# Part 1 of a gated linear attention and FFN kernel in units of two chunks and four heads, with the decays summed on TensorE

## The chip, the cores and the metric

The kernel runs on one core of one Trainium2 chip. The metric is the device time of one execution in microseconds (us). The kernel before takes 508.98 us, median of four runs (507.14 to 509.68). The profiled execution is one of these runs; its span, 506.9 us from the first to the last instruction, is about 2 us shorter than its time.

Runs more than 1.5% above the fastest of their kernel are called slow, and ratios leave them out.

## The reference

```python
# q, k, v, alpha: (B, H, S, D) = (4, 8, 768, 48) float32; alpha in 0.8 .. 1.0
for t in range(S):
    state = alpha[:, :, t, :, None] * state + einsum('bhd,bhe->bhde', k[:, :, t], v[:, :, t])
    y[:, :, t] = einsum('bhd,bhde->bhe', q[:, :, t], state)
x = y.transpose(0, 2, 1, 3).reshape(B * S, H * D)        # 3072 x 384
a, b = x @ w1, x @ w2                                    # w1, w2: 384 x 1024, float64
out = ((a * b) @ w3) @ w_out                             # w3: 1024 x 1024, w_out: 1024 x 384, float64
```

The recurrence is computed in chunks. Within a chunk, `k` is divided by the product of the `alpha`s so far and `q` is multiplied by it; the outputs are then masked scores times `v` (called attend below) plus `q` times the state that enters the chunk. The products of `alpha` are sums of logarithms: a matmul with a triangular matrix of ones, then `exp`. The FFN's matmuls are done with operands split in three parts, and the float64 weights are converted to float32 on the core, on VectorE and ScalarE ("conversions").

## The kernel before

Part 1 is the attention. It goes through 24 units of one chunk (128 positions, one on each partition) with all 8 heads. Between the units it converts the FFN's gate weights (12 blocks) and, from round 5 on, computes gates of token groups that are already finished. Part 2 computes the rest of the gates, folds `w3 @ w_out` and projects.

The loads fetch, for each head and position, the 48 floats of one row, which is 192 bytes:

```python
def rows(src, n):
    b, c = divmod(n, NCH)
    return src[b, :, ds(c * C, C), :].rearrange("h p d -> p h d")     # 192 B runs
```

The sums are one matmul of all 384 features, in two parts (one part, in fp32, in the first ten units), and the decay of the state from chunk to chunk makes a trip by way of DRAM, because it is needed with the features on the partitions and `e` has the positions there:

```python
for i in range(2):
    nc.tensor.matmul(lc, sums[:, n % 2], la[:, i], start=(i == 0), stop=(i == 1))
nc.scalar.activation(e[:, 0], lc, AF.Exp, scale=-1.0)
nc.scalar.activation(e[:, 1], lc, AF.Exp)
if n in ends:                                            # every second chunk
    nc.scalar.dma_start(out=ends[n][0:1], in_=e[0:1, 0])
...                                                      # load_ends: ends -> decs, 4 B runs
```

All psum tiles come from one pool of eight banks. The order of a round is this:

```python
for n in range(N + 1):
    load_v(n + AHEAD - 1); load_a(n + 5); load_kq(n + AHEAD)
    attend_state(n - 1)          # q times the state, into y
    scores(n)
    transposed(n + 1)            # q, k with features on partitions
    ...                          # split_x of a finished group, conversions
    advance(n)                   # decay times state, on GpSimd
    attend(n - 1)                # adds into y; ScalarE copies y out; DMA to DRAM (xd)
    outer(n)                     # k times v, the state's increment
    run(...)                     # a piece of a gate
    decayed(n + 2); logs(n + 4)
    if n in begin: load_x(...)   # a finished group comes back from DRAM
    decays(n + 3); load_ends(n + 2)
```

In these listings calls are put on one line and guards are left out.

## Time and profile before

| | before |
|---|---|
| time, median | 508.98 us |
| TensorE busy | 466.6 of 506.9 us |
| VectorE / ScalarE busy | 371.3 / 248.1 us |
| gaps with no matmul (work is what is left) | 40.2 us |
| TensorE work done at half clock | 18.8 us |
| scores of round 10 / 23 begin at | 106.3 / 205.8 us |

Work and gaps are counted here from the matmul records in the trace: from each matmul's start to the next one's start is work, apart from the time in which no matmul runs, which is a gap. The page's summary lines for the kernel before, and its line for packets and for the queue that carries the loads:

```profile
PE 466.6 (92%) x3760; PEld 424.8 (84%) x3760; DVE 371.3 (73%) x620; ACT 248.1 (49%) x479; POOL 13.8 (3%) x43
...
DMA packets 168735, 79.10 MB, mean 156 GB/s; under 512 B 112856, under 2 KB 162544, under 8 KB 168688
...
q1 hardware_dynamic: 147184, 70.73, 54.9%
```

Two thirds of the packets are under 512 bytes.

### The profile page before, as it was taken

The numbers are of one execution on the slowest core, as the hardware profiler recorded it, in microseconds if no ns is written. First come the engines' busy times: TensorE is split into PE (matmuls) and PEld (weight loads), VectorE is DVE, ScalarE is ACT, GpSimd is POOL, SyncE is SP. The second block draws the span as 40 slices with busy tenths as digits, with TensorE's granted clock in tenths as the row PEclk, the third lists the DMA queues.
The fourth block names the chain that finished last, engine by engine and source line by source line (L and its number), as shares of the span: only waits on it lengthen the run. The fifth ranks groups of instructions, "written<-read, shape, count | busy, mean of one in ns | idle before, by whom it ended". The sixth has DMA issues, their size and how long they took to land.

```text
span 506.9 us, 9883 instructions
## 1 busy us (share of the span) xinstructions
PE 466.6 (92%) x3760; PEld 424.8 (84%) x3760; DVE 371.3 (73%) x620; ACT 248.1 (49%) x479; POOL 13.8 (3%) x43
## 2 busy tenths in 40 slices
PE   3777499499799999999999999999999999999997
PEld 1556388398799899899999998898888799999996
DVE  2777789699966767599999976967533497777771
ACT  2665566468557555355555544544323343333330
POOL 2000000010100010000000000000000000000000
PEclk9998599889899999999999999999999999999999
DMA  9999999998879833265565432432001686555511
GB/s 173 182 217 196 256 216 225 194 246 209 166 167 215 194 81 106 79 186 174 177 200 186 160 117 88 142 103 72 33 31 48 171 231 192 174 180 179 174 56 47
DMA packets 168735, 79.10 MB, mean 156 GB/s; under 512 B 112856, under 2 KB 162544, under 8 KB 168688
## 3 DMA queue, kind: packets, MB, share of 16 engines
q1 hardware_dynamic: 147184, 70.73, 54.9%
q10 hardware_dynamic: 21504, 7.75, 6.7%
q8 instruction: 29, 0.48, 0.4%
q14 instruction: 18, 0.15, 0.1%
HBM read 56.40 MB, written 22.06 MB: 155 GB/s over the span
## 4 chain that ended last, share of the span: by engine, by line
PE 71%; DVE 1%; issue 0%; ACT 0%; DVEq 0%
PE bank L387 36%; PE bank L391 18%; PE bank L436 8%; PE bank L355 2%; PE bank L330 2%; PE bank L430 1%; PE bank L349 1%; PE bank L290 1%; PE bank L302 1%; PE bank L256 1%; DVE x L378 1%; DVE x L377 0%; ACT t L389 0%; ACT ab L454 0%; DVE r L392 0%
## 5 line engine op out<-in xcount | busy, mean ns | idle before, releaser
L387 PE MATMUL bank<-x,w 128*128 128x384 f32 x768 | 163.9, 348 | 15.0 <-DVE x L377 8.5
L387 PEld LDWEIGHTS bank<-x,w 128*128 128x128 f32 x768 | 136.5, 192 | 21.1 <-DVE x L377 9.7
L389 ACT ACTIVATE t<-bank 128x384 f32<-128x384 f32 x152 | 73.4, 490 | 119.2 <-PE bank L387 96.7
L392 DVE SCALAR_TENSOR_TENSOR r<-bank,t 128x384 f32<-128x384 f32 x128 | 68.4, 550 | 45.7 <-ACT t L389 37.1
L391 PE MATMUL bank<-x,w 128*128 128x384 f32 x384 | 89.2, 340 | 1.5 <-DVE x L378 1.4
L391 PEld LDWEIGHTS bank<-x,w 128*128 128x128 f32 x384 | 69.2, 191 | 3.1 <-PE bank L387 1.4
L387 PE MATMUL bank<-w3o,ab 128*128 128x384 f32 x384 | 70.6, 335 | 1.0 <-ACT ab L454 1.0
L387 PEld LDWEIGHTS bank<-w3o,ab 128*128 128x128 f32 x384 | 66.8, 188 | 1.4 <-ACT ab L454 1.3
L436 PE MATMUL bank<-wo,w3T 128*128 128x384 f32 x128 | 42.6, 486 | 0.0
L391 PE MATMUL bank<-w3o,ab 128*128 128x384 f32 x192 | 37.1, 334 | 0.0
L436 PEld LDWEIGHTS bank<-wo,w3T 128*128 128x128 f32 x128 | 24.2, 189 | 14.9
L189 ACT ACTIVATE rest<-raw 128x512 f32<-128x512 uint32 (+1 forms) x36 | 23.4, 649 | 26.6 <-DMA raw<-in_moe_w_dram 18.3
L455 DVE TENSOR_TENSOR ab<-abl,ab 128x1024 fp32r<-128x1024 f32 x24 | 29.4, 1223 | 9.1 <-ACT ab L454 9.1
L403 DVE TENSOR_TENSOR ab<-r 128x384 f32<-128x384 f32 x64 | 35.3, 552 | 0.9
L454 ACT ACTIVATE ab<-abl 128x1024 fp32r<-128x1024 f32 x24 | 25.5, 1062 | 20.1 <-PE bank L391 18.8
L330 PEld LDWEIGHTS bank<-qkT 48*128 48x128 f32 x384 | 25.5, 198 | 10.8 <-ACT qkT L292 5.1
L330 PE MATMUL bank<-qkT 48*128 48x128 f32 x384 | 30.7, 298 | 4.2 <-ACT qkT L292 3.7
L333 DVE TENSOR_TENSOR ms<-bank,keep 128x512 int32<-128x512 int32 x48 | 31.2, 682 | 4.2 <-PE bank L330 4.2
L391 PEld LDWEIGHTS bank<-w3o,ab 128*128 128x128 f32 x192 | 33.6, 188 | 0.0
L292 ACT COPY qkT<-bank 128x512 f32<-128x512 f32 x48 | 25.8, 586 | 10.3 <-PE bank L290 8.8
L194 ACT ACTIVATE power<-power,rebias 128x512 uint32<-128x512 uint32 (+1 forms) x36 | 25.0, 696 | 10.3 <-DVE power L193 10.3
L392 DVE SCALAR_TENSOR_TENSOR o<-bank,t 128x384 f32<-128x384 f32 x24 | 13.4, 556 | 22.1 <-issue 13.7
(65 smaller groups left out, 509.7 us busy)
## 6 DMA issues: line engine op xcount, KB each, us to landing
abd<-ab SPq DMA_DIRECT2D x64, 192.0 KB
abl<-abd SPq DMA_DIRECT2D x24, 512.0 KB
raw<-in_moe_w_dram SPq DMA_DIRECT2D x16, 512.0 KB
raw<-in_moe_w_dram SPq DMA_DIRECT2D x24, 256.0 KB
ac<-in_alpha_dram SPq DMA_DIRECT2D x24, 192.0 KB
kq<-in_k_dram SPq DMA_DIRECT2D x24, 192.0 KB
kq<-in_q_dram SPq DMA_DIRECT2D x24, 192.0 KB
v<-in_v_dram SPq DMA_DIRECT2D x24, 192.0 KB
```

What stands on the lines that cost most here:

```text
L194: nc.scalar.activation(power, power, AF.Relu, scale=2.0 ** 23, bias=rebias)
L292: nc.scalar.copy(qkT[:, :, :, ds(DP * half, DP)], tp[half])
L330: nc.tensor.matmul(sc[i][:, j, :], qkT[r, 0, j, :], qkT[r, 1, j, :], start=True, stop=True)
L333: nc.vector.tensor_tensor(ms[:, i].bitcast(I32), sc[i].bitcast(I32), keep_bc, op=ALU.bitwise_and)
L387: nc.tensor.matmul(p1, w[part][i], x[part][i], start=(part == i == 0), stop=(part == 1 and i == n - 1))
L389: nc.scalar.activation(t, p1, AF.Copy, scale=(1.0 + 1.0 / P) * scale)
L391: nc.tensor.matmul(p2, w[2][i], x[2][i], start=(i == 0), stop=(i == n - 1))
L392: nc.vector.scalar_tensor_tensor(to, p2, -scale, t, op0=ALU.mult, op1=ALU.add)
L403: nc.vector.tensor_mul(ab, *r)
L436: nc.tensor.matmul(po, w3T[:, j, :], wo[:, j, :], start=(j == 0), stop=(j == KF - 1))
L454: nc.scalar.activation(t[:, 0], ab, AF.Copy, scale=1.0 - 2.0 ** -13)
L455: nc.vector.tensor_sub(t[:, 1], ab, t[:, 0].bitcast(FP32))
```

## The change

The intent is threefold: halve the number of load packets, drop the decay's trip through DRAM, and keep TensorE's small matmuls on four quarters of the array at once.

- A unit is now two chunks and four heads. Partition `p` holds positions `2p` and `2p+1` of the pair, so that a run of a load is 384 bytes, and the first chunk lies on partitions 0 to 63, the second on 64 to 127. A chunk is still 128 positions.
- The sums become a matmul over both positions plus corrections of 192 columns each.
- The decays are summed on TensorE directly on the features' partitions: the logarithms are the weights, and a two-column matrix of block indicators is what moves through.
- The outputs `y` get a psum pool of their own, one pair of banks; six banks are left for the rest.
- Scores are computed in two halves, with the attend of the unit before between them.
- Smaller things came along: the gates begin in round 6 in place of 5, the state's matmuls run in all units (with a zero state at the start of a sequence), and the output is stored in two halves.

The diff, cut to its core:

```diff
-    ps = pool("ps", 8, space=PSUM)
+    ps = [pool("ps", 6, space=PSUM)]
+    yp = pool("yp", 2, stack=part1, space=PSUM)
...
-        return src[b, :, ds(c * C, C), :].rearrange("h p d -> p h d")
+        src = src[c // NCH, ds(hh * HH, HH), ds(c % NCH * C, W * C), :]
+        nc.sync.dma_start(out=dst, in_=src.rearrange("h (p r) d -> p h (r d)", r=R))
...
-            for i in range(2):
-                nc.tensor.matmul(lc, sums[:, n % 2], la[:, i], start=(i == 0), stop=(i == 1))
+        for x in parts:
+            nc.tensor.matmul(lc, w[:, 0], x[:, 0:1].to_broadcast([C, R, HH, D]), ...)
+        for x in parts:
+            nc.tensor.matmul(lc[:, 1], w[:, 0], x[:, 1], ...)
+        for x in parts:
+            nc.tensor.matmul(lc[:, 0], w[:, 1], x[:, 1], ...)
+        dec = to[:, DM:DM + NP * W].rearrange("p (j b) -> p j b", b=W)
+        for j in range(NP):
+            for r in range(R):
+                nc.tensor.matmul(dec[:, j], las[n % 2][:, r, 2 * j:2 * j + 2], half, ...)
...
-            nc.scalar.dma_start(out=ends[n][0:1], in_=e[0:1, 0])
+        nc.scalar.activation(decs[n % 6], dec, AF.Exp)
...
+        sc = scores(n)
+        next(sc)                      # first half
+            attend(n - 1)
+        for _ in sc:                  # second half
+            pass
...
+        attend_state(n)               # the state's part of y
+        advance(n + 1)
+        add(n + 1)                    # outer products
+        transposed(n + 1)
```

## The prediction

> **What bounds the kernel now.** I read the page's utilisation rows first, to split the run into stages, then the table of windows to size the idle in each stage, then the timeline of TensorE in a dense stretch to get the price of each kind of work, then the timeline at the holes to see what made them, and the waits last.
>
> ```profile
> PE   3777499499799999999999999999999999999997
> DVE  2777789699966767599999976967533497777771
> PEclk9998599889899999999999999999999999999999
> DMA  9999999998879833265565432432001686555511
> ```
>
> A slice is 12.7 us; I count from 1. From slice 12 on (140 us) PE shows 9 throughout except at the very end: from there the time is TensorE's work and nearly nothing else. The holes (3777, 4, 4, 7) all lie in the first eleven slices, and there the DMA row is at 9 or 8. PEclk dips to 5 in slice 5.
>
> ```profile
> 0.00:20.00 20.00, 8.98 (x64) 5.52 (x66) 7.35 (x15) 7.89 (x15) 2.85 (x19) 1.00 1.13 178
> 20.00:40.00 20.00, 16.52 (x275) 12.82 (x271) 16.08 (x28) 13.92 (x31) 1.16 (x3) 1.00 1.06 203
> 40.00:60.00 20.00, 10.97 (x123) 8.49 (x119) 14.30 (x26) 10.95 (x22) 0.90 (x3) 0.67 1.03 225
> 80.00:100.00 20.00, 12.66 (x184) 10.88 (x183) 14.21 (x25) 11.58 (x25) 0.78 (x2) 0.95 1.01 203
> 120.00:140.00 20.00, 16.53 (x193) 14.80 (x196) 19.17 (x35) 12.72 (x30) 1.96 (x3) 0.91 0.82 182
> ```
>
> Columns: window, its length, busy us of PE, weight loads, DVE, ACT, POOL, then granted clock, DMA share, GB/s. TensorE is idle 11.0, 3.5, 9.0, 7.3 and 3.5 us in these five windows, 34 us together; 60 to 80 and 100 to 120 have under half a microsecond each. In the idle ones the DMA share is 1.13, 1.06, 1.03, 1.01 and 0.82.
>
> ```profile
> 190.80 0.51 PE L256 MATMUL bank<-la,sums 128*128 128x384 f32 x2
> 191.23 0.67 PE L349 MATMUL bank<-qkT,T 48*64 48x128 f32 x16
> 191.83 1.16 PE L330 MATMUL bank<-qkT 48*128 48x128 f32 x16
> 192.83 0.66 PE L290 MATMUL bank<-ident,qk 64*128 64x64 f32 x16
> 193.42 1.09 PE L355 MATMUL bank<-ms,v 128*64 128x128 f32 x16
> 194.34 0.62 PE L302 MATMUL bank<-v,qk 128*64 128x48 f32 x16
> 194.90 1.31 PE L387 MATMUL bank<-x,w 128*128 128x384 f32 x6
> ```
>
> This is one chunk of attention between gate matmuls; start to start are the prices: sums 0.43, state 0.60, scores 1.00, transposes 0.59, attend 0.92, outer products 0.56, together 4.10 us. A plain fp32 matmul stands here as two instructions (8 score matmuls, x16).
>
> ```profile
> 92.18 0.60 PEld L302 LDWEIGHTS bank<-v,qk 128*64 128x64 f32 x16
> 95.53 0.43 DVE L190 TENSOR_SCALAR mant<-raw 128x512 uint32<-128x512 uint32 x1 [4.75 <-DMA raw<-in_moe_w_dram]
> ```
>
> Here DVE, in order, stands 4.75 us in front of a weight block that has not landed; behind it wait the split of x and so the gates. The same hole is at 52.4 to 57.2. So the stage is held by transfers that arrive late, and by the in-order engines that stand before them.
>
> ```profile
> POOL dec L319 <- DMA dec<-ends: 156.4, 8, 28.3
> DVE mant L190 <- DMA raw<-in_moe_w_dram: 13.0, 4, 4.8
> ```
>
> The first is the trap: 156.4 us, but POOL has nothing else to do. What it holds up is only T, for which PEld waits 3.0 us in all. Removing the trip by way of DRAM is by itself worth little.
>
> **What the Trainium skill says.** "DMA: Bandwidth & Descriptors", Specifications: line rate needs 512 B and more. In the trace the 98,304 packets of 192 B took 17.7 ns each in mean (10.8 B/ns), the 33,792 of 512 B 30 ns (17 B/ns): it agrees. "TensorE: Matmul & The Clock Gate", LDWEIGHTS: columns over 1.2 ns, whatever the rows. The two loads of 128 columns of L253 at 36.68 us span 0.30 us with 0.19 for one, so 0.11 apart: 107 ns, agreed. The same page, What's actually happening: the clock falls to half after an idle window of about 3.4 us. The clock records have half speed for 17, 7 and 3 us, each around one of the holes: agreed. "TensorEngine Tiling (Array Packing)", Key Properties: changing the tiling mode drains the array. In the chunk above each of the four changes of shape costs some 0.2 us over the pure stream (0.60 for the state against 16/4 x 0.109 = 0.44): it agrees.
>
> **The change, part by part.** There are 24 units before and after, 25 rounds of the loop.
>
> Transfers: q, k, v, alpha go from 98,304 packets of 192 B to 49,152 of 384 B. Between 17.7 and 30 ns I take 25 ns (an estimate, linear in size): 77 us of sixteen engines in place of 109. With the 9,216 four-byte packets of the decays (9 ns, 5 us) some 37 us of 176 go. Per unit the inputs cost 3.2 us in place of 4.5. The share in 20 to 120 us should fall from 1.0 to about 0.8.
>
> TensorE, per unit, streams at the paces above. Scores and attend are 32 instructions each now, but on four 64x64 tiles at once, where the trace has 27 ns (L349): 0.87 and 0.87, in place of 0.90 and 0.87. State 0.44 in all 24 units, before in 20. Outer products 32 instructions of 48 columns; a pair took 58 ns on two tiles, so four tiles give 32/4 x 58 = 0.47 (0.23 in the last pair of units), mean 0.39, as before. Transposes 0.50, unchanged. Sums: two matmuls of 384 columns (0.173) and four of 192, which the weight load bounds at 0.112: 0.79 in place of 0.35; in fp32 (first ten units) 1.3 in place of 0.65. New: the decays on the features' partitions, 4 matmuls of two columns, 8 instructions, each behind a load of 128 columns: 8 x 0.108 = 0.86. Changes of shape: three in place of four, 0.6 for 0.8. Sum 5.3 against 4.17 (5.8 against 4.5 early). Over 24 units 1.15 x 24 = 28 us more TensorE work. This is the price, and nothing hides it where PE is at 9.
>
> DVE: two adds of 96 columns in place of one of 192, some 0.15 us per unit, 3 us in all. ACT: 24 exps of four columns, an estimated 5 us; 40 issues of DMAs at 0.3 us go, 12 us. Gates, folds and the projection do not change.
>
> What it gives back: before, fixed work is (1152 + 576) x 0.1733 for gates and projection, 128 x 0.322 and 64 x 0.109 for the fold: 348 us. Attention is 24 x 4.17 + 10 x 0.3 = 103. The rest of 506.9, 56 us, is loss: idle, half clock, cold start, tail. After: fixed 348, attention 24 x 5.3 + 10 x 0.5 = 132, so 480 without loss. Of the loss some 20 stays whatever comes: 11 until the first unit runs, 4 of cold clock there, 5 at the tail. The holes of 4 to 9 us with their half clock should go: rounds 5, 9 and 13 took 18.6, 17.4 and 12.0 us (score to score), others some 7.3 to 8.4, so 9 to 10, 9 and 4, some 23 us. What remains beyond: the splits at five groups of gates (0.8 each, 4 us) and the rounds before the gates, where DVE (0.95 + 1.36 + 0.5 + 3 to 4 steps of conversion at 1.07, 6 to 7 us) binds rather than TensorE (5.9). That leaves a loss of about 25 us: a span of 505, and the time before stood 2 us above its span.
>
> By rounds as a check: first scores at 15, six rounds at 6.4 to 53, eighteen at 5.3 + 3.2 of gates, less 5 for those without sums, plus 2 extra pieces and four at the end: some 212 with 42 half gates done, against 212 with 39 before. Three half gates are 4.7 us. The change then ends 0 to 5 us ahead. I say 505.
>
> **Rivals.**
> First, the transfers were everything and TensorE's extra work falls into its idle. For it: DMA at 1.0 with PE at 0.5. Against it: only 34 us are idle before 200, 11 of them at the start, and 20 us of the extra work lies in rounds that are dense. Its best case has a loss of 12 to 15: 494 to 497.
> Second, the holes stay because other waits take their place: psum falls to six banks for eleven tiles a round (eight for twelve), and DVE has 7.3 us of work in a round of 8.5. Then TensorE pays 28 us and recovers 10 to 15: 520.
> Third, the sums cost less than I say, if the two-column matmuls overlap their loads: up to 15 us less, 492. Against: the 107 ns between loads of 128 columns.
>
> **Range and chances.** The middle is 505; the loss could be 16 to 36 us, so 496 to 516 holds it eight times in ten. Faster by over 2% (below 498.7) needs the first or third rival: 0.21. Slower by over 2% (above 519.1) needs the second in full: 0.11. Within 2%: 0.68.
>
> **What would show it.** The DMA row below 9 from slice 2 to 9; no wait of several us of DVE for raw; PEclk without the 5. The decay line with 192 instructions at 0.11 us pace, sums at 0.8 a unit, a round of 8.5 us between scores. The lines of the second half unchanged. I am wrong if packets of 384 B take 30 ns or more, if TensorE waits for banks, or if a dense round is nearer 7.5 us.

## The result, and the profile after

The changed kernel takes 536.41 us, median of four runs (533.73 to 540.12), against 508.98. The ratio is 1.055, with a 95% interval of 1.0481 to 1.0619. It is 5.5% slower, and 31 us above the prediction. Ratios here and below are the mean time of one kernel's fast runs over that of the kernel before's of the same rounds, so they are not quite the ratio of the medians.

The profiled execution is the fastest of the four. From its page, first the busy times, then the rows in 40 slices (13.3 us each), then packets and the loads' queue:

```profile
PE 503.9 (95%) x5200; PEld 467.2 (88%) x5200; DVE 378.3 (71%) x642; ACT 253.8 (48%) x503; POOL 32.8 (6%) x61
...
PE   5988797899999999899999999999999999999996
...
DVE  3697999955645755448999999877643487667771
...
PEclk8998998999899999799999999999999999999999
DMA  8979886665455432213765555241001676556622
...
DMA packets 115260, 79.23 MB, mean 149 GB/s; under 512 B 54784, under 2 KB 109056, under 8 KB 115200
...
q1 hardware_dynamic: 101216, 70.73, 45.3%
```

The transfers went as intended: 53,475 packets fewer, the queue's share down from 54.9 to 45.3%, the DMA row below 9 in all slices but two. The 4s in PE's row are gone. And yet PE is busy 37.3 us longer. Stage by stage, from the matmul records (all in us; the stages are cut where the scores of rounds 0, 10 and 23 begin; the 15 us until round 0 are left out, and the last stage ends 4 us after the last matmul):

| stage | before: length | work | gaps | after: length | work | gaps |
|---|---|---|---|---|---|---|
| rounds 0 to 10 | 90.9 | 70.6 | 20.3 | 92.2 | 79.7 | 12.5 |
| rounds 10 to 23 | 99.5 | 95.2 | 4.3 | 122.9 | 117.7 | 5.3 |
| after that | 301.1 | 296.4 | 1.0 | 302.0 | 297.7 | 0.1 |

In the first ten rounds the change won 7.8 us of gaps and paid 9.1 us of work, with nine gate matmuls fewer done by then. In the next thirteen it paid 22.5 us of work and there were no gaps to win. (Some 3 us of these are the clock: 9.8 us of the work there ran at half clock, before 3.3.) Of the work, by kind, start to start over the whole run:

| kind | before | after | prediction |
|---|---|---|---|
| decays | none | 21.4 | 20.6 more |
| sums | 17.0 | 28.7 | some 12.7 more |
| outer products | 11.3 | 16.9 | none more |
| scores, attend, transposes, state | 79.6 | 80.3 | 3 less (1.8 more for the state, 4.8 less for changes of shape) |
| gates, fold, projection | 358.6 | 356.7 | the same |

In the kernel after, the outer products and the state's matmuls run mixed, so that the split between these two rows is uncertain by some 2 us; their sum is not. Work counted in this way also holds waits too short to show as a gap, as the next lines show.

A dense round of the kernel after, on TensorE; columns are start, length, engine, line, operation, output and inputs, shapes, count:

```profile
153.03 0.51 PE L276 MATMUL bank<-la,sums 128*128 128x384 f32 x2
153.38 0.36 PE L279 MATMUL bank<-la,sums 128*128 128x192 f32 x2
153.58 0.39 PE L281 MATMUL bank<-la,sums 128*128 128x192 f32 x2
153.80 0.97 PE L286 MATMUL bank<-half,la 128*128 128x2 f32 x8
154.71 0.67 PE L347 MATMUL bank<-qkT 48*64 48x128 f32 x16
155.19 1.05 PE L401 MATMUL y<-ms,v 64*48 64x128 f32 x32
156.07 0.62 PE L347 MATMUL bank<-qkT 48*64 48x128 f32 x16
156.80 0.73 PE L390 MATMUL y<-qkT,T 48*64 48x128 f32 x13
157.28 0.26 PE L364 MATMUL bank<-v,qk 64*64 64x48 f32 x2
157.36 0.28 PE L390 MATMUL y<-qkT,T 48*64 48x128 f32 x3
157.38 0.71 PE L364 MATMUL bank<-v,qk 64*64 64x48 f32 x14
158.02 0.71 PE L331 MATMUL bank<-ident,qk 64*128 64x64 f32 x16
```

Start to start: sums 0.77, decays 0.91, first scores 0.48, attend 0.88, second scores 0.73, state and outer products together 1.22, transposes 0.64 to the gates at 158.66. The next round's first scores stand at 163.60, so a round is 8.89 us; before it is 7.3. Look at the lines L390 and L364: the scheduler has set the outer products (shape 64*64) in among the state's matmuls (48*64), where the program has one after the other. And look at what lies before them, with ScalarE's line from the same stretch:

```profile
156.29 0.65 ACT L409 COPY x<-y 128x256 f32<-128x256 f32 x2
```

The last score matmul starts at 156.42, and the state's first only at 156.80, where 0.09 us is the step from attend to scores. The state's matmuls write the two `y` banks, and ScalarE's copies of the unit before out of these banks end at 156.66 and 156.93; the first matmuls into the one and the other bank start at 156.80 and 156.99. In all dense rounds from 10 to 21 it is the same, to 0.1 us. The table of waits below doesn't list this wait: with the ends that the profile models for matmuls, a gap of some 0.1 us is left of it.

In the first ten rounds the windows of the kernel after (window, length, busy us of PE, weight loads, DVE, ACT, POOL, then granted clock, DMA share, GB/s) say:

```profile
20.00:40.00 20.00, 18.14 (x404) 16.20 (x404) 17.07 (x35) 13.95 (x33) 6.34 (x8) 1.00 0.85 241
40.00:60.00 20.00, 16.58 (x300) 14.53 (x300) 16.81 (x30) 13.27 (x29) 0.06 (x1) 0.91 0.96 272
60.00:80.00 20.00, 17.64 (x314) 16.01 (x314) 19.91 (x39) 13.30 (x30) 4.97 (x4) 1.00 0.78 225
80.00:100.00 20.00, 16.13 (x280) 15.17 (x279) 19.90 (x42) 13.05 (x31) 3.83 (x4) 0.91 0.61 173
```

From 60 to 100 us VectorE is busy 39.8 of 40 us, while TensorE has holes and the DMA share is at 0.78 and 0.61. The hole at 84 us, in the timeline of all engines:

```profile
85.46 0.42 DVE L216 TENSOR_SCALAR power<-raw 128x512 uint32<-128x512 uint32 x1
...
85.91 0.72 ACT L217 ACTIVATE power<-power,rebias 128x512 uint32<-128x512 uint32 x1 [1.49 <-DVE power L216]
...
86.98 0.63 ACT L409 COPY x<-y 128x256 f32<-128x256 f32 x2
...
87.48 0.73 PE L390 MATMUL y<-qkT,T 48*64 48x128 f32 x13 [3.01 <-ACT x L409]
```

Read from the bottom: the state's matmuls wait 3.01 us for their one pair of `y` banks, which ScalarE frees by copying the unit before out. ScalarE is in order, and stands before that copy at a conversion step, which waits 1.49 us for VectorE, which is full of conversions. In the table of waits (what waited, for what, us in total, times, longest) this is the new kind, and the waits for weights have shrunk:

```profile
ACT rest L212 <- DMA raw<-in_moe_w_dram: 13.2, 10, 2.7
...
PE y L390 <- ACT x L409: 10.7, 8, 3.0
...
DVE mant L213 <- DMA raw<-in_moe_w_dram: 1.4, 1, 1.4
```

Before, the two waits for raw weights stood at 18.3 and 13.0 us. VectorE is fuller in these rounds because the scheduler drew the conversions of the weights forward: counted in VectorE's compiled order, 7 gate blocks are converted by unit 8 and 9 by unit 10 in the kernel before, and 11 and 12 in the kernel after.

### The profile page after: what moved, and what is told of

It reads as the page before. It is cut to its first block, busy times and chain, and to the rows that moved or that the text cites. A ratio compares the mean times of both kernels' runs of the same rounds, so it can differ in the third digit from the quotient of the medians.

```text
span 531.9 us, 12881 instructions
## 1 busy us (share of the span) xinstructions
PE 503.9 (95%) x5200; PEld 467.2 (88%) x5200; DVE 378.3 (71%) x642; ACT 253.8 (48%) x503; POOL 32.8 (6%) x61
## 3 DMA queue, kind: packets, MB, share of 16 engines
q1 hardware_dynamic: 101216, 70.73, 45.3%
## 4 chain that ended last, share of the span: by engine, by line
PE 58%; DVE 0%; issue 0%; DVEq 0%
PE bank L443 31%; PE bank L447 16%; PE bank L492 8%; PE bank L486 1%; PE y L401 1%; PE bank L347 1%; PE y L390 0%; PE bank L331 0%; PE bank L364 0%; DVE o L448 0%; DVEq L448 0%
## 5 line engine op out<-in xcount | busy, mean ns | idle before, releaser
L443 PEld LDWEIGHTS bank<-x,w 128*128 128x128 f32 x768 | 134.2, 189 | 9.2 <-DVE x L433 3.2
L448 DVE SCALAR_TENSOR_TENSOR r<-bank,t 128x384 f32<-128x384 f32 x128 | 69.6, 556 | 56.0 <-ACT t L445 40.9
L447 PEld LDWEIGHTS bank<-x,w 128*128 128x128 f32 x384 | 69.3, 191 | 3.4 <-PE bank L443 3.4
L334 ACT COPY qkT<-bank 128x512 f32<-128x512 f32 x48 | 25.7, 587 | 28.4 <-PE bank L331 21.4
L297 DVE TENSOR_TENSOR qk<-kq,e 128x768 f32<-128x768 f32 x24 | 23.1, 964 | 18.5 <-ACT e L292 18.3
L510 ACT ACTIVATE ab<-abl 128x1024 fp32r<-128x1024 f32 x24 | 25.5, 1061 | 18.8 <-PE bank L447 12.5
L347 PE MATMUL bank<-qkT 48*64 48x128 f32 x768 | 32.4, 284 | 0.0
L212 ACT ACTIVATE rest<-raw 128x512 f32<-128x512 uint32 (+1 forms) x36 | 23.4, 651 | 18.0 <-DMA raw<-in_moe_w_dram 13.2
L217 ACT ACTIVATE power<-power,rebias 128x512 uint32<-128x512 uint32 (+1 forms) x36 | 25.1, 699 | 13.8 <-DVE power L216 13.6
L306 POOL TENSOR_TENSOR dec<-dec,dec 128x2 f32<-128x2 f32 x16 | 21.1, 1319 | 164.3 <-ACT dec L293 135.4
```

The source lines that it names most:

```text
L217: nc.scalar.activation(power, power, AF.Relu, scale=2.0 ** 23, bias=rebias)
L334: nc.scalar.copy(qkT[:, b], tp[b].rearrange("p i j r c -> p i j (r c)"))
L347: nc.tensor.matmul(sc[i][rows(b), s, j, :], qkT[f, b, 0, j, rows(s)], qkT[f, b, 1, j, :], start=True, stop=True)
L443: nc.tensor.matmul(p1, w[part][i], x[part][i], start=(part == i == 0), stop=(part == 1 and i == n - 1))
L447: nc.tensor.matmul(p2, w[2][i], x[2][i], start=(i == 0), stop=(i == n - 1))
L448: nc.vector.scalar_tensor_tensor(to, p2, -scale, t, op0=ALU.mult, op1=ALU.add)
```

## The experiments

Three ideas compete. The expectations call the first one theory 1: TensorE streams more, nothing hides it, and the time follows. Its rival: the added work would mostly fall into idle time, and what costs is new waits, on the one pair of `y` banks and on the in-order engines. The third is about VectorE: its order of conversions. Each run carries a ratio to the kernel before; one hundredth is 5.1 us.

### Taking the decays away, and putting their DRAM trip back

Without the decays' matmuls and their `exp`; values are wrong:

```diff
-        for j in range(NP):
-            for r in range(R):
-                nc.tensor.matmul(dec[:, j], las[n % 2][:, r, 2 * j:2 * j + 2], half, ...)
-        nc.scalar.activation(decs[n % 6], dec, AF.Exp)
+    for x in decs:                       # once, at the start
+        nc.gpsimd.memset(x, 0.05)
```

> The changed kernel without its decay matmuls (4 of two columns a unit) and their exp; the decays are a constant, so the result is wrong on purpose. Theory 1, the price (the added TensorE streaming sets the time, and the 21.4 us that these 192 instructions hold TensorE are paid in full): 515 us, 20 to 22 below the changed kernel's 536, with the round between scores down from 8.9 to 8.0 us. Theory 2, the waits (the time is lost to waits for the y banks behind DVE's and ACT's queues, and the added matmuls mostly fill idle): 530 or more, TensorE idle up by about what its work falls.

528.02 us (527.2 to 529.05), ratio 1.0409. Some 7 us came back where 21 us of decays went: TensorE's work fell by 15.4 us, gaps rose from 28.0 to 38.7 us, and in the waits of this run the state's matmuls now wait 16.3 us for the copy of `y` in place of 10.7. Theory 1 in its plain form falls for this layout: another limit lies close behind the work.

The decays by way of DRAM again, in the new layout (correct):

```diff
-        nc.scalar.activation(decs[n % 6], dec, AF.Exp)
+        if n in ends:
+            nc.scalar.dma_start(out=ends[n][0:1], in_=e[0:1, 0, 0])
+        if n + 2 in ends:
+            nc.scalar.dma_start(out=ends[n + 2][1:2], in_=e[C - 1:C, R - 1, 1])
+    # load_ends(n + 2) as before, in units of the new layout
```

> The changed kernel with the decays by way of DRAM again, as the kernel before had them, everything else as changed; the result is right. Theory 1: like the run without decays, 515 us, because the trip by way of DRAM holds up nothing (before, TensorE waited 3 us in all for it). If the trip was a cost worth removing, as the change supposes: 525 or more, with TensorE waiting for T. Theory 2: 530 or more.

543.26 us (540.91 to 544.19), ratio 1.0701. So in this layout the sums on TensorE are the better of the two ways: 1.5 hundredths better than the trip they replace. The trip costs 15 us over the run without any decays, with the waits for `y` up to 19.8 us; the prediction's "by itself worth little" was read off the old layout, where it is needed half as often.

### Relief and price in the old layout

The kernel before with loads of 384-byte rows, in the same number of transfers; the rows that arrive are not the right ones, so values are wrong, but nothing else changes:

```diff
-        return src[b, :, ds(c * C, C), :].rearrange("h p d -> p h d")
+        s = src[b, ds(c % 2 * (H // 2), H // 2), ds(c // 2 * 2 * C, 2 * C), :]
+        return s.rearrange("h (p r) d -> p h (r d)", r=2)
```

> The kernel before with its loads of q, k, v and alpha in packets of 384 B (other rows of the inputs than it should have, so the result is wrong on purpose; all else unchanged). It tells what the relief of the transfers is worth alone. My prediction's step (the holes of rounds 5, 9 and 13 go, 23 us): 486 us. If other waits take the place of the transfers at once, as in the changed kernel, where TensorE's idle fell by only 12 us and the work at half clock stayed at 20 us: 495 to 502. If the transfers were hidden anyway: 507 to 509.

499.19 us (496.68 to 500.37), ratio 0.9823. This is the relief of the loads alone: 9 us, where the prediction counted on 31 given back in all. Rounds 5, 9 and 13, which the prediction wanted to shrink from 18.6, 17.4 and 12.0 us by 23 us in all, took 16.4, 14.4 and 12.3 us. The timeline of this run shows what holds round 5 when the transfers no longer do:

```profile
47.06 0.39 ACTq L374 DMA_DIRECT2D xT<-xd  x1
...
53.63 1.16 ACT L380 ACTIVATE x<-xT 128x1152 fp32r<-128x1152 f32 x1 [2.74 <-DMA xT<-xd]
...
54.84 2.72 PE L391 MATMUL bank<-x,w 128*128 128x384 f32 x6 [6.20 <-ACT x L380]
```

The first group of gates needs `x`, which comes back from DRAM: asked for at 47.06, used at 53.63, and TensorE stands for 6.20 us. In the kernel before the same load is asked for at 47.49 and the gates start at 57.20. The hole is the round trip of `x` and its split, with the weights in the way only in part.

The opposite: the kernel before plus as many two-column matmuls a chunk as the decays need, results unread (correct):

```diff
+        for i in range(4):
+            nc.tensor.matmul(to[:, ds(DM + 2 * i, 2)], raw[:, ds(i % 3 * C, C)], utri[:, 0:2],
+                             start=False, stop=True, skip_group_check=True)
```

> The kernel before with 4 fp32 matmuls of two columns a chunk added, behind loads of 128 columns, whose output nobody reads (right result). Theory 1: most of 24 x 0.9 = 21 us is paid, less what falls into the holes of the first rounds: 520 to 528. Theory 2: they fall into idle, 509 to 514.

523.72 us (521.1 to 524.25), ratio 1.0312: 16 us for 26 us of such work, within the range of theory 1. In the old layout most of the added work is paid, and the rest fell into gaps, which went from 40.2 to 29.0 us.

### More room for y, and the order of state and outer products

Four banks for `y` and four for the rest (correct):

```diff
-    ps = [pool("ps", 6, space=PSUM)]
+    ps = [pool("ps", 4, space=PSUM)]
-    yp = pool("yp", 2, stack=part1, space=PSUM)
+    yp = pool("yp", 4, stack=part1, space=PSUM)
```

> The changed kernel with four psum banks for y instead of two, so that two units' outputs can stand there, and four in place of six for the rest (alternating with none). In the run without decay matmuls TensorE's idle rose from 24 to 35 us, nearly all of the rise in front of the state matmuls, which wait for ACT's copy of the unit before out of the only pair of y banks. Theory 2a (this one pair of banks ties TensorE to ACT's and DVE's queues): the 11 to 12 us before the state matmuls go, 522 to 526. If four other banks are too few, the waits move to them: 534 to 540. Theory 1 (price alone): 533 or more.

549.77 us (543.01 to 552.85, one slow run), ratio 1.0858: a miss, and the wrong way. The wait did not go away, it moved: no matmul into `y` is in this run's table of waits any more, and the transposes stand for a bank instead.

```profile
PE bank L331 <- DVE ms L352: 16.8, 21, 3.0
```

The same with the decays removed (wrong), and with the two positions' logarithms added on GpSimd first so that the decays need half the matmuls (correct, with one buffer less for `v` to make room):

> Without decay matmuls (wrong result on purpose) and with four y banks. Theory 2a: with the banks freed the removal is paid out, 21 us below the run with four y banks alone and some 20 below the run without decay matmuls alone: 503 to 508. If DVE's queue (19.9 of 20 us busy from 60 to 100 us) is a bound by itself, behind which TensorE waits wherever the bank is: 515 to 522.

> Four y banks, and the decays from sums of the two positions made on POOL first, so 2 matmuls a unit in place of 4 (right result; one buffer of v less, for room). If a decay matmul costs its 0.22 us: 10 us below the run with four y banks alone, 512 to 516. If the decay matmuls are hidden: as that run.

533.53 us (ratio 1.0522) and 542.89 us (ratio 1.0663, the profiled run slow): both far above what was hoped, with 22.4 and 20.4 us of waits of the transposes for a bank. With four banks for everything else the banks bind. Against the run with four `y` banks alone (1.0858), though, they are 17 and 10 us faster by ratio, give or take 3 to 4 us. So in this layout, where nothing waits for `y`, most of the decays' 23.8 us of work comes back when it is removed, and most of a half when that is; with one pair of `y` banks it was 7 us.

The outer products ahead of the state's matmuls (correct):

```diff
-        attend_state(n)
         advance(n + 1)
         add(n + 1)
+        attend_state(n)
         transposed(n + 1)
```

> The changed kernel with only the order of two pieces changed: the outer products of the next unit before the state matmuls, which gives ACT 0.65 us more to clear the y banks. Theory 2a: waits of 1 to 3 us shrink by 0.65 each, of some ten of them: 529 to 532. Theory 1: 536.

529.2 us (526.93 to 534.62), ratio 1.0448, one hundredth better than the kernel after. The dense round of this run shows why:

```profile
157.34 0.62 PE L347 MATMUL bank<-qkT 48*64 48x128 f32 x16
157.77 0.62 PE L364 MATMUL bank<-v,qk 64*64 64x48 f32 x16
158.23 0.68 PE L390 MATMUL y<-qkT,T 48*64 48x128 f32 x16
158.84 0.71 PE L331 MATMUL bank<-ident,qk 64*128 64x64 f32 x16
```

From the second scores to the transposes it is 1.50 us, against 1.95 in the kernel after (156.07 to 158.02), with the same 48 matmuls, and the round is 8.4 us in place of 8.9. Two things differ, the mixing and the wait for `y`, and the trace tells them apart. ScalarE's copies end just as late after the last score matmul (0.24 and 0.51 us), and in both kernels the state's last matmul starts 0.96 us after it. But here the outer products run in the wait, from 0.09 to 0.50, where in the kernel after they come last, up to 1.46. So the 0.45 us are the outer products' own 0.46, moved into the wait for the copy; the expectation had this in kind, and its range of 529 to 532. The mixing of shapes costs next to nothing. Here the outer products take 0.46 us (in this trace and the next ones 16 of them on two tiles or 32 on four alike), where the prediction said 0.47, and 0.23 for the last pair of units.

### The order of the conversions

The conversions' instructions on VectorE and ScalarE kept in the program's order, so that the scheduler can't draw them forward (correct); 8 of 12 gate blocks are then converted by unit 10:

```diff
-        nc.vector.scalar_tensor_tensor(mant, top, 2.0 ** -20, rest, op0=ALU.mult, op1=ALU.add)
+        tc.keep_in_program_order(nc.vector.scalar_tensor_tensor(mant, top, 2.0 ** -20, rest, ...))
         # and so for all ten instructions of the conversions
```

> The changed kernel with the steps that convert the weights held to the place where the program puts them (8 gate weights before unit 10; the scheduler of the changed kernel drew 12 ahead of it, that of the kernel before 9, and DVE was busy 103.6 of the first 107.0 us against 84.6 of 106.3). Theory 3 (DVE's order: the scheduler filled the time that the transfers gave back with conversions, and TensorE waits in the first ten rounds for DVE and, behind it, for ACT): unit 10 starts at 95 to 100 us in place of 107, total 525 to 530, unless the later conversions hold up the second part. Theory 1 (price alone): the first ten rounds stay at 105 to 108, 535.

528.47 us in median (525.88 to 537.86), ratio 1.0321. Two of the six runs were slow, the profiled one among them, so no stage is read from it. (The 103.6 and 84.6 us of VectorE in the expectation count overlapping records twice; without the overlap they are 90.4 and 75.8 us.) Pinning gives 2.3 hundredths back. Then the same without the decays (wrong), and with the outer products ahead (correct):

> The same without decay matmuls (wrong result on purpose). Without the pin their removal gave 8 of 21 us and nothing in the first ten rounds (108.4 us). Theory 3: with DVE out of the way the removal pays in the first rounds too: unit 10 at 88 to 93 us, total 505 to 512. If TensorE still waits elsewhere: 515 or more.

> The changed kernel with the conversions held to their place and with the outer products before the state matmuls (which by itself gave 7 us). Theory 3: the two add up in part, 518 to 524; TensorE's idle below 18 us. What then remains above the kernel before is the price of TensorE's added streaming.

523.39 us, ratio 1.027; and 528.23 us in median with a profiled run of 524.08, ratio 1.0232. The second fell in two heaps, 519 and 524 against 532 twice, which count as slow. In both the scores of round 10 begin at 96 and 98 us, where the kernel after has 107.0: the first ten rounds were held by VectorE's order and the copy of `y` behind it. But the decays, once more, gave back only half a hundredth when removed (1.0321 to 1.027, each with an interval of 0.005 either way).

So, still with both mended, once more without the decays (wrong):

> Wrong values on purpose. The kernel after with the conversions kept in program order and the outer products ahead of the state's matmuls, and without the decay matmuls. Theory 1 (what is left once the waits are out of the way is streamed work, so the decays now cost all they stream): 20 us below the same kernel with decays, whose fast runs lie at 519 to 524: 500 to 506. Rival (one wait or another always fills the room, as in the three removals so far, which paid 8, 16 and 5 us): 512 or more.

517.49 us (516.94 to 518.98), ratio 1.0181. The rival comes nearer: half a hundredth for the 21 us that the decays stream. The ratio with decays rests on two fast runs and reaches from 1.0147 to 1.0317; the two profiled runs lie 7 us apart. Rounds 10 to 23 took 118.8 us without the decays and 119.3 with them. Work fell by 5.9 us there, gaps rose from 5.8 to 11.2 us, and 13.6 us of the work ran at half clock in place of 10.0. Round by round it is not one limit: rounds 10, 12, 15, 18 and 20 fell from 8.4 us to 7.6 or 7.7, nearly all that the decays stream, and rounds 13 and 14 together, 16 and 19 grew by 0.6, 1.0 and 1.4 us. In rounds 13 and 16 the state's matmuls stand for `y` (1.83 and 1.42 us), in round 19 a gate for a bank (1.68 us). In the waits of this run it is mostly the same pair of banks again, at twice the 4.7 us of the run with decays:

```profile
PE y L385 <- ACT x L404: 9.9, 7, 2.7
```

With only the conversions of part 1 pinned, so that those of part 2 may move (correct):

> Correct. As the kernel with pinned conversions and the outer products ahead, but with only the conversions of part 1 pinned, so that those of the second half may move again. If the small holes that stood in the fold came from the pinned second half, the time is 515 to 520 and TensorE idle falls by 2 to 4 us; if not, 519 to 524 or 532 as before.

521.08 us in median (517.05 to 532.62, one slow run), ratio 1.0242. Gaps fell from 24.4 to 22.0 us, as expected, and the time, just above the expected 515 to 520, is the same within the intervals as with everything pinned. This is the best correct version of the new layout that was found.

### The control, which came out unexpected

Everything pinned in the kernel before (correct):

> Correct. A control: the kernel before with its conversions pinned the same way. Before, the transfers hold the first ten rounds and VectorE has room, so that its order should matter little: 505 to 512. If pinning by itself speeds up any layout by 8 us (499 to 502), then its gain in the kernel after says nothing of what the change did.

533.47 us (532.81 to 535.51), ratio 1.0498, 25 us slower; and both expected ranges missed. The scores of round 23 began at 198.6 us, 7 us earlier than without the pin. From there to the end it took 332.9 us, against 301.1: the 7 us and 25 more went in part 2, where the fold now waits for its weights (21.8 us more of gaps), and 17.4 us of the work run at half clock, none before:

```profile
PE bank L430 <- DVE w L199: 21.8, 7, 6.0
```

So the pin in part 1 helps the kernel before as well, and its gain in the kernel after can't all be charged to the change. Pinned in part 1 alone (correct):

```diff
+    pinned = [True]
+    def kept(x):
+        return tc.keep_in_program_order(x) if pinned[0] else x
     ...
     part1.close()
+    pinned[0] = False
```

> Correct. The kernel before with only the conversions of part 1 pinned. With all of them pinned it was 7 us ahead when the scores of round 23 began (198.6 against 205.8) and lost 32 us in the second half, where the fold waited for VectorE. If the two are separate, this one keeps the first and loses nothing: 499 to 503, and it beats both kernels. If the gain of part 1 is paid back in the second half, 507 or more.

502.47 us (501.33 to 503.12), ratio 0.988, interval 0.9856 to 0.9905. It beats both kernels, correctly, by an edit that has nothing to do with the change. And with the wide loads besides (wrong):

> Wrong rows on purpose. Wide loads and pinned conversions of part 1 together in the kernel before. If they mend different holes, they add: 490 to 494. If they mend the same ones, 497 to 501.

496.03 us (494.49 to 497.27), ratio 0.9763, between the two expectations: pinned, the wide loads give 1.2 hundredths in place of 1.8; or the other way round, the pin gives 0.6 in place of 1.2. They mend partly the same holes.

### Adding the work up in the relieved old layout

The kernel before with wide loads and the decay-sized matmuls (both edits above; wrong), and then with the extra pieces of sums too, as matmuls with zero weights:

```diff
+            for i in range(4):
+                s = ds(i // 2 * DM // 2, DM // 2)
+                nc.tensor.matmul(lc[:, s], zero, la[:, i % 2, s], start=False, stop=(i == 3), ...)
             # in the first ten units: two such pieces in fp32
```

> Wrong rows on purpose. The kernel before with the wide loads and with the same number of decay-sized matmuls a chunk, results unread: relief and price together in the old layout. Theory 1 (both add up: -9 and +16): 513 to 518. Rival (the relieved stage has idle that takes the added work in): 505 or less. In either case it lies well below the 536 of the kernel after, the rest being sums, outer products and the waits of the new layout.

> Wrong rows on purpose. The kernel before with the wide loads, the decay-sized matmuls and as many extra pieces of sums as the kernel after has (with zero weights): relief and nearly all of the added TensorE work, in the old layout and with eight shared banks. Theory 1 (streamed work adds to the time): 512.8 and 8 to 12 more, 521 to 525; what then remains to the 536 of the kernel after is the outer products and the waits of the new layout. Rival (the sums fall into idle): 516 or less, and the waits of the new layout are most of the loss.

512.81 us (509.17 to 515.49), ratio 1.008; and 519.63 us (516.46 to 521.08), ratio 1.0211. Both came out just below the ranges of theory 1 (513 to 518, 521 to 525) and above those of its rival (505 or less, 516 or less). In the old layout, with transfers relieved and eight shared banks, the added decays cost 13 us and the added sums 7. The 13 us stand against 24.6 us of such matmuls in the trace, and gaps fell from 31.1 to 23.4 us: the relieved layout takes in a part, and roughly half is paid.

## Why the prediction was wrong

It said 505, by two sums: 28 us more work on TensorE (29 with what it adds for the early units), and 31 us given back. The profiled spans have 37 us more work (467 to 504) and 12 us fewer gaps (40.2 to 28.0). Both terms failed, and the second by more.

**The price, 28 us, was mis-sized; it measured 37.** The decays (20.6 said, 21.4 measured) and the sums (12.7 said, 11.7 measured) were right to 1 us. The step that failed is "Outer products … as before" together with "Changes of shape: three in place of four, 0.6 for 0.8": outer products and the other small matmuls took 6.3 us more, in place of 3 less. The prediction laid a unit's streams end to end and had no wait between them. In the traces the state's matmuls stand for ScalarE's copy of `y`, and the outer products come behind them: 0.45 us in each of the dense rounds 10 to 21, 5.4 us in all. Moving the outer products into that wait brought a dense round from 8.9 to 8.4 us, under the 8.5 that was predicted. What is left of the 9 us, some 3 to 4, is not assigned. The price of a change of shape was misread besides: the streams that the prediction gives add up to some 3.5 of the 4.10 us of its own stretch, which leaves 0.6 us for all boundaries and not 0.8 for four.

**The give-back, 31 us, is the step that failed most.** "The holes of 4 to 9 us with their half clock should go" rested on reading the holes of rounds 5, 9 and 13 as late weight blocks. The wide loads alone, in the old layout, shortened these three rounds by 4.9 us and not 23, and the run by 9. The hole of round 5 there is the trip of `x` through DRAM and its split on in-order engines. In round 5 TensorE's longest gap went from 4.78 to 6.20 us with the wide loads; the "same hole" of the prediction was not the weights'. The hole of its fence, in round 9, was in part: there VectorE's wait for a weight block fell from 4.75 to 1.91 us, and TensorE's gaps from 6.6 to 3.6. Work done at half clock, which should have gone, is 20.0 us in the kernel after, against 18.8; the 5 in the PEclk row is gone, but the half clock is spread over more stretches. Nor do these stretches agree with the idle window of about 3.4 us that the prediction names: at 143.5 us the clock fell with TensorE idle for 1.0 us of the 3.4 before.

**The second rival was right in kind.** "The holes stay because other waits take their place" is what the traces show, with the state's matmuls waiting for `y` (10.7 us, and the short waits of the dense rounds besides) behind ScalarE and a VectorE that was full from 60 to 100 us. It expected 520, because it paid 28 us of work; with 37 of work and 12 recovered, and a profiled run 2.7 us under the median, the measured 536 follows. It had been given 0.11.

**What was right:** the packets. The prediction took 25 ns for one of 384 bytes; in the trace of the kernel after, the 49,152 of them took 23.8 ns in mean. "No wait of several us of DVE for raw" came true (1.4 us in all), and the DMA row was below 9 from slice 2 to 9 but for two slices. Transfers were relieved, and in the old layout that alone was worth 9 us; most of the holes did not hang on them.

The path from one kernel to the other, in ratios (times 508.7 us). It goes through the old layout first, and each line is the difference of two measured ratios:

| step | from, to | us |
|---|---|---|
| wide loads | 1 to 0.9823 | -9.0 |
| decays' matmuls | 0.9823 to 1.0080 | +13.1 |
| extra pieces of sums | 1.0080 to 1.0211 | +6.7 |
| outer products behind the state's matmuls, not in their wait for `y` | 1.0448 to 1.0550 | +5.2 |
| order of the conversions: what pinning gives in the new layout (1.0448 to 1.0242) less what it gives in the relieved old one (0.9823 to 0.9763) | | +7.4 |
| not assigned | | +4.6 |
| sum | 1 to 1.0550 | +28.0 |

The intervals of the ratios reach 0.002 to 0.007 either way, that is 1 to 3.5 us for each of the ratios in a line, and the lines depend on the order in which they are taken. One point stays open: the decays cost 13 us when added to the old layout but give back only 3 us when removed from the new one with its order mended (7 between the profiled runs). The traces of that pair say that plain rounds give it back and a few rounds lose it again, mostly to waits for the one pair of `y` banks. With four `y` banks 17 us came back, which speaks for that pair of banks as the reason; it is not a clean test, because with eight banks in all the transposes then ran short. The 4.6 us also stay open, with the smaller parts of the change that were not tried apart.

## What to carry to other kernels

Before a hole is booked as a gain, follow it past the first wait in the timeline, and ask what TensorE would wait for if that one were gone: a cheap version of the relief alone, with wrong data, measures it. Work added to the busiest engine was paid nearly in full in the rounds without gaps (0.8 us a round, added or removed) and in part elsewhere, and taking it away need not pay it back where another wait lies close behind. A short wait in every round hides in "busy" and in no table of waits: compare the last start of one kind with the first of the next, and put other work into it. When a tile scheduler orders the engines, compare the compiled order of both kernels, not the programs: here it drew conversions forward, and an order kept on purpose was worth 1.2% even to the kernel before.

## What the Trainium skill lacked or had wrong

- "TensorE: Matmul & The Clock Gate", Wait — 56ns, not 53.3ns?: it says that start to start never drops below about 25 ns. Matmuls on different tiles of the array are an exception that is not named there (the same page's part on packing has some 4 ns between tiles): in the dense rounds here the scores come in fours, 6 to 8 ns apart and then mostly 88 to 94, and with the conversions pinned and the outer products ahead, 32 outer products on four tiles took 0.46 us, 14 ns each.
- "TensorEngine Tiling (Array Packing)", Key Properties: it says that a change of tiling mode drains TensorE but gives no price. With the outer products ahead, it is 0.20 us from the last state matmul (48*64) to the first transpose (64*128), and 0.09 from attend to scores, both on tiles of 64 by 64, which is no more than the step inside them. The same tiles with half the matmuls are no faster: 16 outer products on two tiles took 0.46 us too.
- "DMA: Bandwidth & Descriptors", Specifications: it gives 512 B as the size for line rate, but the page has no measured time of a packet of 192 to 512 bytes. Here a packet took 17.7 ns at 192 B, 23.8 at 384 B and 30 at 512 B.
- No page was found that tells how the scheduler's order of in-order engines moves waits from one engine to another. Pinning ten instructions moved the kernel before by -1.2% in part 1 alone and by +5.0% when part 2 was pinned too.
